# Agent attention into two expert layers on one core: the first product of layer 1 contracts over 128 rows in the place of 113

## The chip, the cores and the metric

The kernel runs on one core of one Trainium2 chip. The metric is the time of the execution on the device in microseconds (us). In this text PE is TensorE (its weight loads are shown apart, as PEld), DVE is VectorE, ACT is ScalarE, POOL is GpSimd and SP is SyncE, whose queue issues the large transfers.

## The reference

There are 12480 tokens of 128 channels and 49 agents. Attention runs first from the agents to the keys, then from the queries to the agents; two feed-forward layers with 2048 hidden units follow.

```
a2k = softmax(agents @ k.T / sqrt(128));  agent_v = a2k @ v          # 49 x 128
q2a = softmax(q @ agents.T / sqrt(128));  x = q2a @ agent_v          # 12480 x 128
h1  = relu(x @ w_in);   y = (s * h1 * h1 + b) @ w_out                # layer 1
h2  = relu(y @ w_in2);  out = (h2 * h2) @ w_out2                     # layer 2
```

## The kernel before

**Layer 1 from the agents.** Since `x @ w_in` is `q2a @ (agent_v @ w_in)`, the kernel forms `M = agent_v @ w_in` once (49 agents by 2048 hidden units) and layer 1 starts from the softmax weights themselves. Most products run on pairs of tiles: a value is split into a high part and a low remainder, and three products (low by high, high by low, high by high) are summed. In the first product of layer 1 the two parts of the softmax weights stand in one tile `X`: rows 0 to 48 hold one part and rows 64 to 112 the other, with rows 49 to 63 zero. `M` has the same layout, `Mh` the high parts and `Ml` the low ones, each once in rows 0 to 48 and again in rows 64 to 112. So two matmuls (`Ml` by `X`, `Mh` by `X`) do what would be four. The number of rows that they contract over is `KS = GAP + NA = 64 + 49 = 113`.

**Where the layout comes from.** `av` (high and low, 128 channels by 113 columns) holds the normalised agent values twice, at columns 0 and 64, on a ground of zeros that POOL writes at the start. `m_piece(i)` multiplies it with 512 hidden units of `w_in` (three matmuls, L338) into PSUM tile `ps_M`, and `split` (L112 on ACT, L113 on DVE) writes the pieces of `Mh` and `Ml`. There are four pieces: two before the main loop, two in steps 2 and 3. `q_stack(t)` transposes the softmax weights of a block of tokens into `ps_x` (L223) and copies its halves into the `X` tile of that block; there are two such tiles, which POOL sets to zero at the start (L378).

**The main loop.** The tokens lie in 28 blocks, 27 of 448 and a last one of 384. A block takes 8 steps (`NPR`), a step handles two of the 16 chunks of hidden units, and the steps of all blocks follow one another (`st`). In each step PE gets, in the order of the code:

- `up1(t, i)` (L543): 4 matmuls, `Ml` by `X` then `Mh` by `X` for two chunks, into a two-bank tile `ps_h`
- in some steps the work of another block: `q_transpose` (`ps_q`, L141) and `q_scores` (`ps_s`, L167) while the block to come is one of the first six, `q_scores_T` (`ps_sT`, L177, step 1) and `q_back` (`ps_b`, L192, step 2) for later ones, and `q_stack` (`ps_x`, L223) in step 6
- `up2` (L554): 6 matmuls of layer 2 for a block that is 11 steps behind, weights `wi2`
- `down` of layer 1 (L565 with `wo`): 6 matmuls; `down` of layer 2 (L565 with `wo2`): 6 matmuls
- after step 5 the four transposes of the output (`ps_o`, L592)

So a plain step is 22 matmuls with 128 by 448 or 113 by 448 moving elements: 4 at L543, 6 at L554, 12 at L565. `hidden` empties each `ps_h` tile: ACT takes relu (L530) and square (L531), DVE the split (L112, L113). The order on every engine is that of the code, written out by hand. After the last block's `up1` the loop drains: steps with L554 and L565 alone are left.

Of the kernel before, what the change touches and what calls it, by code (L numbers as in the profile page):

```python
# [10 lines left out]
F32R = mybir.dt.float32r  # L11
# [5 lines left out]
P = 128  # L17
# [21 lines left out]
def tile_agent_attention_two_moe(  # L39
# [14 lines left out]
    nc = tc.nc  # L54
    _, N, C = q.shape
    NA = agents.shape[1]
    DFF = w_in.shape[1]
# [4 lines left out]
    KS = GAP + NA  # L62
# [23 lines left out]
    const = ctx.enter_context(tc.tile_pool(name="const", bufs=1))  # L86
# [5 lines left out]
    ident = const.tile([P, P], F32, name="ident")  # L92
    ones = const.tile([P, P], F32, name="ones")
    aT = const.tile([P, GAP], F32, name="aT")
    M = [const.tile([KS, DFF], F32R, name=f"M{x}") for x in "hl"]
    av = [const.tile([P, KS], F32R, name=f"av{x}") for x in "hl"]
    s_sb = const.tile([P, 1], F32, name="s_sb")
    b_sb = const.tile([P, 1], F32, name="b_sb")
    ones_r = const.tile([P, P], F32R, name="ones_r")
# [5 lines left out]
    sTs = [const.tile([KS, 256], F32, name=f"sT{i}") for i in range(2)]  # L105
    aS = const.tile([P, KS], F32R, name="aS")
    halves = (0, slice(0, NA)), (1, slice(GAP, KS))
    Xs = [const.tile([KS, 512], F32R, name=f"X{i}") for i in range(2)]

    def split(dst, src, eng_lo, copy=nc.vector.tensor_copy):  # L110

        copy(dst[0], src)  # L112
        eng_lo.tensor_tensor(out=dst[1], in0=src, in1=dst[0].bitcast(F32), op=ALU.subtract)  # L113


    q_raw, qT, q_sT, q_e, q_st, X = {}, {}, {}, {}, {}, {}
# [216 lines left out]
    def m_piece(i):  # L333

        sl = slice(i * WC, (i + 1) * WC)
        ps = ps_m.tile([P, 512], F32, tag="m", name="ps_M")
        for z, (x, w) in enumerate(((av[0], wi[1]), (av[1], wi[0]), (av[0], wi[0]))):
            nc.tensor.matmul(out=ps[:KS], lhsT=x, rhs=w[:, sl], start=(z == 0), stop=(z == 2))  # L338
        split((M[0][:, sl], M[1][:, sl]), ps[:KS], nc.vector, nc.scalar.copy)

    with tc.manual_schedule():

        with tc.tile_pool(name="pre", bufs=1) as pre, tc.tile_pool(name="kp", bufs=2) as kp:
# [42 lines left out]
            ps = ps_m.tile([P, 512], F32, tag="m", name="ps_w")  # L386
            for i in range(16):
                nc.tensor.transpose(out=ps[:, :P], in_=ident, identity=ident)
            ps = ps_m.tile([P, 512], F32, tag="m", name="ps_a")
# [51 lines left out]
            ps = ps_m.tile([P, 512], F32, tag="m", name="ps_mt")  # L441
# [7 lines left out]
            ps = ps_m.tile([P, 512], F32, tag="m", name="ps_mb")  # L449
# [36 lines left out]
            for g, (_, p, j) in enumerate(kblocks):  # L486
# [6 lines left out]
                for i in range(j):  # L493
                    nc.tensor.matmul(
                        out=ps_av[:NA, :C + 1],
                        lhsT=S[:p, t0[g] + i],
                        rhs=vs[g][:p, i],
                        start=(g == 0 and i == 0),
                        stop=(g == NG - 1 and i == j - 1),
# [9 lines left out]
            ps = ps_m.tile([P, 512], F32, tag="m", name="ps_avT")  # L509
# [4 lines left out]
            for c0 in (0, GAP):  # L514
                nc.vector.tensor_tensor(
                    out=av[1][:, c0:c0 + NA], in0=ps[:, :NA], in1=av[0][:, c0:c0 + NA].bitcast(F32), op=ALU.subtract
                )
            for i in range(2):
                m_piece(i)
                fill(FM[i])  # L520
# [16 lines left out]
        def up1(t, i):  # L537
            n = blocks[t][1] * blocks[t][2]
            ps = ps_h.tile([P, 2, 512], F32, tag="h", name="ps_h1")
            for c in range(2):  # L540
                sl = slice((2 * i + c) * P, (2 * i + c + 1) * P)
                for z in (1, 0):
                    nc.tensor.matmul(out=ps[:, c, :n], lhsT=M[z][:, sl], rhs=X[t], start=(z == 1), stop=(z == 0))  # L543

# [54 lines left out]
        for st in range(total + L2 + LAG + 3):  # L599
            t, i = divmod(st, NPR)  # L600
# [8 lines left out]
            if st in M_AT:  # L609
                m_piece(2 + M_AT.index(st))  # L610
# [19 lines left out]
            t, i = divmod(st - L2, NPR)  # L630
            if 0 <= t < NB:
                up2(t, i)
            t, i = divmod(st - LAG, NPR)
# [4 lines left out]
            t, i = divmod(st - L2 - LAG, NPR)  # L638
# [4 lines left out]
            t, i = divmod(st - L2 - LAG - NPR, NPR)  # L643
# [32 lines left out]
```

## Time and profile before

| | |
|---|---|
| median of 3 runs | 1139.34 us (1139.15 to 1139.51) |
| the profiled execution | 1138.89 us |
| its span, first to last instruction | 1136.9 us |
| PE busy | 1113.1 us, 98% of the span |
| DVE, ACT busy | 979.4 and 943.5 us (86% and 83%) |
| mean granted TensorE clock | 0.993 of full speed |
| chain that ended last | PE 87%: L565 45%, L554 24%, L543 15% |

The span lies 2.0 us below the execution's own time, and the profiled execution 0.45 us below the median. Matmuls are pipelined, so a matmul's own duration is longer than the distance from its start to the start of the next one. That distance is called the pitch below; a group's pitch is read from the starts of two rows and the number of matmuls between them. In the chain view the durations of a group already add up to the distance between rows.

### The profile page before, as it was taken

How to read it: one execution, taken by the hardware profiler on the slowest of the kernel's cores; microseconds unless marked ns; L12 is line 12 of the kernel's file. 1: busy time of each engine (PE TensorE's matmuls, PEld its weight loads, DVE VectorE, ACT ScalarE, POOL GpSimd, SP SyncE). 2: the span in 40 equal slices, each digit the busy share in tenths (PEclk: the TensorE clock that was granted, in tenths of full speed). 3: DMA queues.
4: the chain of work that ended last, by engine and by line, in shares of the span. 5: the costliest groups of instructions: out<-in, count | busy, mean ns of one | idle time of the engine just before them, and what ended most of it. 6: DMA issues, size and time to landing. Idle time of an engine off the chain costs nothing.

```text
span 1136.9 us, 15468 instructions
## 1 busy us (share of the span) xinstructions
PE 1113.1 (98%) x5787; PEld 1026.2 (90%) x5787; DVE 979.4 (86%) x1425; ACT 943.5 (83%) x1183; POOL 38.3 (3%) x45
## 2 busy tenths in 40 slices
PE   8997899999999999999999999999999999999998
PEld 8986799999999999999999999999999999999997
DVE  5889998888888888888888888888888888888875
ACT  4646798888888888888888888888888888888875
POOL 1226100000000000000000000000000000000000
PEclk9899999999999999999999999999999999999999
DMA  8861009999999999999999999999999999800000
GB/s 309 246 200 35 1 1 23 15 15 7 15 15 15 13 10 15 15 15 8 15 15 15 7 15 15 15 15 8 15 15 15 8 15 15 12 1 9 9 10 15
DMA packets 1285730, 34.96 MB, mean 31 GB/s; under 512 B 1255239, under 2 KB 1281752, under 8 KB 1285656
## 3 DMA queue, kind: packets, MB, share of 16 engines
q1 hardware_dynamic: 1285368, 33.98, 116.0%
q8 instruction: 45, 0.74, 0.4%
q14 instruction: 29, 0.24, 0.1%
q10 hardware_dynamic: 288, 0.00, 0.0%
HBM read 27.58 MB, written 6.39 MB: 30 GB/s over the span
## 4 chain that ended last, share of the span: by engine, by line
PE 87%; DVE 6%; ACT 1%; issue 1%; POOL 0%; DVEq 0%; ACTq 0%
PE ps_y L565 45%; PE ps_h L554 24%; PE ps_h L543 15%; PE ps_o L592 1%; PE ps_sT L177 1%; DVE gh L112 1%; DVE gl L113 0%; ACT r L530 0%; DVE x L273 0%; DVE x L279 0%; DVE li L275 0%; PE ps_x L223 0%; POOL gl L113 0%; PE ps_b L192 0%; DVE ex L281 0%
## 5 line engine op out<-in xcount | busy, mean ns | idle before, releaser
L530 ACT ACTIVATE r<-ps_h 128x896 f32<-128x896 f32 (+1 forms) x448 | 408.7, 912 | 109.0 <-PE ps_h L543 77.7
L113 DVE TENSOR_TENSOR gl<-r,gh 128x896 fp32r<-128x896 f32 (+1 forms) x439 | 477.5, 1088 | 15.1
L531 ACT ACTIVATE r<-r 128x896 f32<-128x896 f32 (+1 forms) x448 | 426.6, 952 | 14.3
L112 DVE CAST gh<-r 128x896 fp32r<-128x896 f32 (+1 forms) x448 | 281.1, 628 | 108.8 <-ACT r L531 97.0
L554 PE MATMUL ps_h<-yh,wi2l 128*128 128x448 f32 (+1 forms) x448 | 169.1, 378 | 2.3 <-DVE yh L112 1.6
L565 PE MATMUL ps_y<-gl,woh 128*128 128x448 f32 (+1 forms) x448 | 163.3, 365 | 5.9 <-POOL gl L113 5.3
L543 PE MATMUL ps_h<-X,Ml 113*128 113x448 f32 (+1 forms) x448 | 166.4, 371 | 0.8 <-DVE Ml L113 0.8
L554 PE MATMUL ps_h<-yl,wi2h 128*128 128x448 f32 (+1 forms) x448 | 163.6, 365 | 0.1
L554 PE MATMUL ps_h<-yh,wi2h 128*128 128x448 f32 (+1 forms) x448 | 163.6, 365 | 0.0
L543 PE MATMUL ps_h<-X,Mh 113*128 113x448 f32 (+1 forms) x448 | 163.5, 365 | 0.0
L565 PE MATMUL ps_y<-gh,wol 128*128 128x448 f32 (+1 forms) x448 | 163.3, 364 | 0.0
L565 PE MATMUL ps_y<-gl,wo2h 128*128 128x448 f32 (+1 forms) x448 | 162.4, 362 | 0.6 <-DVE gl L113 0.6
L565 PE MATMUL ps_y<-gh,woh 128*128 128x448 f32 (+1 forms) x448 | 162.6, 363 | 0.0
L565 PE MATMUL ps_y<-gh,wo2l 128*128 128x448 f32 (+1 forms) x448 | 162.4, 362 | 0.0
L565 PE MATMUL ps_y<-gh,wo2h 128*128 128x448 f32 (+1 forms) x448 | 161.8, 361 | 0.0
L565 PEld LDWEIGHTS ps_y<-gl,woh 128*128 128x128 f32 x448 | 84.5, 189 | 13.5 <-POOL gl L113 6.8
L554 PEld LDWEIGHTS ps_h<-yh,wi2l 128*128 128x128 f32 x448 | 84.4, 188 | 9.7 <-issue 1.9
L554 PEld LDWEIGHTS ps_h<-yl,wi2h 128*128 128x128 f32 x448 | 84.9, 190 | 6.9 <-DVE yl L113 0.6
L543 PEld LDWEIGHTS ps_h<-X,Ml 113*128 113x128 f32 x448 | 84.5, 189 | 7.3 <-issue 1.2
L554 PEld LDWEIGHTS ps_h<-yh,wi2h 128*128 128x128 f32 x448 | 84.3, 188 | 7.0
L565 PEld LDWEIGHTS ps_y<-gh,wol 128*128 128x128 f32 x448 | 84.5, 189 | 6.4 <-ACT y L573 0.4
L565 PEld LDWEIGHTS ps_y<-gl,wo2h 128*128 128x128 f32 x448 | 84.1, 188 | 6.7 <-DVE gl L113 1.2
(122 smaller groups left out, 1025.5 us busy)
## 6 DMA issues: line engine op xcount, KB each, us to landing
kraw<-in_k_dram SPq DMA_DIRECT2D x12, 512.0 KB, 7.7
v<-in_v_dram SPq DMA_DIRECT2D x12, 512.0 KB, 7.3
q_raw<-in_q_dram SPq DMA_DIRECT2D x27, 224.0 KB, 36.3
out_dram<-o SPq DMA_DIRECT2D x27, 224.0 KB, 2.8
raw<-in_moe_w_in_dram SPq DMA_DIRECT2D x8, 512.0 KB, 7.0
raw<-in_moe_w_out_dram SPq DMA_DIRECT2D x8, 512.0 KB, 5.4
q_raw<-in_q_dram SPq DMA_DIRECT2D x1, 192.0 KB, 31.7
out_dram<-o SPq DMA_DIRECT2D x1, 192.0 KB, 2.3
```

Source lines behind the costliest of these rows:

```text
L112: copy(dst[0], src)
L113: eng_lo.tensor_tensor(out=dst[1], in0=src, in1=dst[0].bitcast(F32), op=ALU.subtract)
L177: nc.tensor.matmul(out=ps[:KS, :n], lhsT=aS, rhs=x[z][:, :n], start=(z == 1), stop=(z == 0))
L530: nc.scalar.activation(r[:, :, :n], ps[:, :, :n], AF.Relu)
L531: nc.scalar.activation(r[:, :, :n], r[:, :, :n], AF.Square)
L543: nc.tensor.matmul(out=ps[:, c, :n], lhsT=M[z][:, sl], rhs=X[t], start=(z == 1), stop=(z == 0))
L554: nc.tensor.matmul(out=ps[:, c, :n], lhsT=w[:, sl], rhs=y[:, :n], start=(z == 0), stop=(z == 2))
L565: nc.tensor.matmul(out=py[t][:, :n], lhsT=wz[:, m], rhs=g[:, c, :n], start=(m == 0 and z == 0), stop=(m == NCH - 1 and z == 2),)
L592: nc.tensor.transpose(out=po[:, i], in_=x[:, i * p:(i + 1) * p], identity=ident)
```

## The change

`M` and `X` become tiles of 128 partitions, `av` gets 128 columns. The zeros that POOL wrote on columns 49 to 63 of `av` and on rows 49 to 63 of `X` now also stand on columns and rows 113 to 127. `m_piece` computes all 128 rows of `M` (the new ones are zero) and splits them. Every matmul of `up1`, whose text is unchanged, then has 128 rows in the place of 113; the sums are the same.

```
-    M = [const.tile([KS, DFF], F32R, name=f"M{x}") for x in "hl"]
-    av = [const.tile([P, KS], F32R, name=f"av{x}") for x in "hl"]
+    M = [const.tile([P, DFF], F32R, name=f"M{x}") for x in "hl"]
+    av = [const.tile([P, P], F32R, name=f"av{x}") for x in "hl"]
...
-    Xs = [const.tile([KS, 512], F32R, name=f"X{i}") for i in range(2)]
+    Xs = [const.tile([P, 512], F32R, name=f"X{i}") for i in range(2)]
...
-            nc.tensor.matmul(out=ps[:KS], lhsT=x, rhs=w[:, sl], start=(z == 0), stop=(z == 2))
-        split((M[0][:, sl], M[1][:, sl]), ps[:KS], nc.vector, nc.scalar.copy)
+            nc.tensor.matmul(out=ps, lhsT=x, rhs=w[:, sl], start=(z == 0), stop=(z == 2))
+        split((M[0][:, sl], M[1][:, sl]), ps, nc.vector, nc.scalar.copy)
```

## Rows read from the trace of the kernel before

**Rows 1.** The page: its span, then busy time of three engines.
```profile
span 1136.9 us, 15468 instructions
...
PE 1113.1 (98%) x5787; PEld 1026.2 (90%) x5787; DVE 979.4 (86%) x1425; ACT 943.5 (83%) x1183; POOL 38.3 (3%) x45
```
**Rows 2.** Waits of PE, 130 to 1090 us: total us, times, longest.
```profile
PE ps_h L554 <- ACT r L530: 0.5, 1, 0.5
```
**Rows 3.** Chain that ended last, one block: start us, us, what.
```profile
504.35 0.81 PE ps_h L543 x4
...
505.36 1.22 PE ps_h L554 x6
...
508.98 0.82 PE ps_h L543 x4
509.80 1.23 PE ps_h L554 x6
511.02 2.40 PE ps_y L565 x12
513.42 0.82 PE ps_h L543 x4
...
519.23 1.23 PE ps_h L554 x6
```
**Rows 4.** The same chain where the loop drains.
```profile
1097.62 1.23 PE ps_h L554 x6
...
1101.09 1.20 PE ps_h L554 x6
...
1109.17 1.20 PE ps_y L565 x6
...
1117.72 1.06 PE ps_h L554 x6
...
1119.81 1.04 PE ps_h L554 x6
```
**Rows 5.** Timeline of PE early in the loop: start us, us of one.
```profile
89.86 0.37 PE L565 MATMUL ps_y<-gh,wol 128*128 128x448 f32 x1
...
91.10 0.36 PE L543 MATMUL ps_h<-X,Ml 113*128 113x448 f32 x1
```
**Rows 6.** The chain in one of the first blocks.
```profile
147.52 0.73 PE ps_s L167 x8
148.26 1.29 PE ps_h L554 x6
149.55 2.47 PE ps_y L565 x12
152.03 0.81 PE ps_h L543 x4
...
156.54 0.81 PE ps_h L543 x4
```
**Rows 7.** One group by form, 130 to 280, then 280 to 1090 us: busy, mean ns.
```profile
L565 PE MATMUL ps_y<-gl,wo2h 128*128 128x448 f32 x64 | 23.4, 365 | 0.0
...
L565 PE MATMUL ps_y<-gl,wo2h 128*128 128x448 f32 x352 | 127.6, 363 | 0.0
```
**Rows 8.** Weight loads by line and form: busy us, mean ns of one.
```profile
L543 PEld LDWEIGHTS ps_h<-X,Mh 113*128 113x128 f32 x448 | 84.9, 190 | 5.2
L554 PEld LDWEIGHTS ps_h<-yl,wi2h 128*128 128x128 f32 x448 | 84.9, 190 | 6.9 <-DVE yl L113 0.6
...
L338 PEld LDWEIGHTS ps_M<-wo2l,avh 128*113 128x113 f32 x4 | 0.7, 176 | 1.1 <-PE ps_y L565 1.0
```
**Rows 9.** POOL's memsets by line: busy us, mean ns of one.
```profile
L378 POOL MEMSET X<- 113x512 f32 x2 | 1.0, 526 | 0.0
L376 POOL MEMSET stack<- 128x256 f32 x2 | 0.6, 314 | 0.0
L376 POOL MEMSET sT<- 113x256 f32 x2 | 0.6, 311 | 0.0
```

## The prediction, made before the changed kernel ran

> **What bounds the kernel now.** I read the page first. PE is busy for 1113.1 of 1136.9 us; DVE and ACT stand at 86% and 83% [rows 1]. Next the waits of PE: in the 960 us from 130 to 1090 us there is one, of 0.5 us [rows 2]. So in the loop no other engine and no transfer holds PE back, and only what PE itself spends on a matmul can move the time. That is not a matter of busy time, which is full anyway; it is the pitch, so I read the chain that ended last as a clock. A plain step (the step at 508.98 us) is 0.82 us for four matmuls at L543, 1.23 for six at L554, 2.40 for twelve at L565, and the next step starts 4.44 us after this one [rows 3]. Per matmul that is 0.205, 0.205 and 0.200 us, although all 22 stream 448 columns. The question for this change is why the ten matmuls at L543 and L554 are slower than the twelve at L565, and whether the 113 rows are the cause.
>
> Three stretches bear on that. First, the drain: behind the last block's `up1` no L543 stands between the groups, and there six matmuls at L554 take 1.20 us, 0.200 each, as do six at L565 (at 1101.09 and 1109.17) [rows 4]. One step earlier, still right behind a group at L543, the same line took 1.23 (at 1097.62) [rows 4]. Second, before layer 2 has begun, a group at L565 comes right behind L543: six matmuls of 128 rows take 91.10 - 89.86 = 1.24 us [rows 5]. So the excess of 0.03 us is neither a property of L554 nor of the tile it writes: it falls on whatever stands behind L543. Third, a bad sign, one of the first blocks: behind eight small products (`ps_s`, L167) twelve matmuls at L565 take 2.47 us, 0.206 each, and the next step is again 4.51 us long (152.03 to 156.54) while L543 itself takes 0.81 [rows 6]. PE can thus run 128-row matmuls at 0.200 or at 0.206 us, and it stays with one of them for many matmuls. The later blocks hardly know the slow pitch: one group of L565 lasts 365 ns in the mean from 130 to 280 us and 363 from 280 to 1090 [rows 7]. What decides between the two I can't read from the trace.
>
> **The change part by part.**
>
> *L543, 224 steps, the last 8 of them 384 columns wide.* No instruction is added or removed. The rows go from 113 to 128. Bounds: if rows cost nothing, the pitches stay: 0. If the excess behind and inside L543 comes from the switch between 113 and 128 rows, a plain step falls to the price of an undisturbed stream, 22 x 0.200 = 4.40 us [rows 4], 0.04 less than now. The rows of the drain and of the early step are the nearest to an all-128-row loop, and I take the second value.
>
> A block has five steps with the plain sequence (0, 3, 4, 5, 7): 5 x 0.04 = 0.20 us. In the three others small products stand between L543 and L554, and these keep their fewer rows or columns. Behind transposes L554 has an excess without any L543 near: in the drain 1.06 against 1.04 us (at 1117.72 and 1119.81) [rows 4]. So of the 1.22 us behind `ps_x` (at 505.36) [rows 3], and behind `ps_b` alike, no more than about 0.01 can go. With 0.01 for each L543 group of 0.81 us (at 504.35) [rows 3], and up to 0.03 behind `ps_sT` (at 519.23), the three steps give 0.02 to 0.07; I take 0.04. The block gives 0.24 us.
>
> Blocks 5 to 26 repeat one pattern: 22 x 0.24 = 5.3 us. In blocks 0 to 4, where steps of both pitches occur [rows 6, 7], the gain lies between 0 and 5 x 0.24 = 1.2 us; I take half, 0.6. The last block and the drain give nothing. Sum: 5.9 us.
>
> *A rule against it.* The weight load of L543 with 113 rows takes 190 ns, that of L554 with 128 rows also 190 [rows 8]. The Trainium skill, page "TensorE: Matmul & The Clock Gate", section "LDWEIGHTS (loading the stationary operand)", says that the load's time goes with the columns of the stationary operand and not with its rows, and its section "Back-to-back issue gap" gives the spacing of matmuls as a function of the moving columns alone. By that rule this change moves nothing and the time stays 1139.3 us; by the rows above it is 5.9 us less. The trace agrees with the rule for the load, and disagrees with it for the spacing, by 2.5% between L554 behind L543 and L554 in the drain.
>
> *`m_piece`.* Twelve matmuls get 128 stationary columns in the place of 113. Their weight loads take 176 ns, those with 128 columns 190 [rows 8]: at most 12 x 0.014 = 0.17 us if none were hidden behind the stream of 512 columns; I take 0. The evictions keep 512 columns and get 15 more partitions. Partitions cost POOL nothing measurable (314 ns for 128, 311 for 113 at 256 columns) [rows 9]; ACT and DVE I take to be the same, 0.
>
> *POOL's start.* `X` keeps its columns; the two `av` memsets get 15 more columns, at 526/512 ns a column 0.015 us each [rows 9]. Cover: these tiles are first used some 75 us later. Without the cover it would be 0.03 us.
>
> *What is late next.* At 4.40 us a step PE still leads: 979.4 us of DVE work and 943.5 of ACT lie below the 1131 us that the span would have [rows 1], and in the loop neither holds PE now.
>
> *Against the runs.* The profiled execution took 1138.89 us, 2.0 more than its span; 1138.89 - 5.9 = 1133.0. It lay 0.45 below the median, so the forecast for the median is 1139.34 - 5.9 = 1133.4 us.
>
> **The rivals.**
>
> *A, rows cost nothing:* the excess comes from something else that only L543 brings (the same `X` streamed four times, one more group per step that waits for a `ps_h` tile). For it: the weight loads show no difference between 113 and 128 rows [rows 8], and streams of 128 rows at 0.206 exist. The Trainium skill's rule above speaks for it too. Against it: L554 also waits for a `ps_h` tile in the drain and has no excess. Time 1139.3 us.
>
> *B, the slow pitch takes hold:* the change removes the group that now stands between streams of 128 rows. In the slow step L543 costs 0.81 us, less than 4 x 0.206 = 0.82, and the fast pattern comes back behind L543 in every step of the later blocks; it may be what brings it back. If PE falls to 0.206 behind a small product and nothing pulls it out, a step is 22 x 2.47/12 = 4.53 us, 0.13 above the clean one [rows 6]. Place: the steps between the small products, from `ps_x` or `ps_b` on. The point from which it decides: 0.24/(8 x 0.13), or 23% of the steps, makes the gain zero. Half the steps slow gives (4 x 0.13 - 0.24) x 22 = +6.2 us, 1145.5 us; all of them (8 x 0.13 - 0.24) x 22 = +17.6, 1157 us. For it: the slow pitch is there in the first blocks and outlasts four steps. Against it: the whole drain, 128-row matmuls only, holds 0.200 behind waits and transposes, and from 280 us on the mean at L565 leaves hardly any room for slow groups [rows 7].
>
> *C, the change reaches further than I count:* the excess goes from the three mixed steps too, 8 x 0.04 x 27 = 8.6 us: 1130.7 us. The excess behind transposes in the drain speaks against it.
>
> **How the numbers follow.** A measurement of this kernel tells about 0.2% (2.3 us) from no change. The forecast and C are faster by more: 0.58 together (C 0.06). A, with the cases of B that land near zero: 0.20. B beyond that: 0.22, spread from 1141.6 to 1157. The range must reach from the faster cases over A into B until no more than 2 in 10 is left out: 1131 to 1144 us, where 1144 is B with some four steps in ten slow. It leaves out about 0.14 of B's chance above and 0.03 of C's below. The likeliest case alone has 1131 to 1136: its bounds are 22 x 0.22 + 0 and 22 x 0.27 + 1.2 us of gain, with about a microsecond for runs that differ.
>
> **What the profile after would show.** Right: plain steps of 4.40 us, L543 0.80 and L554 1.20 in the chain, the mean duration of L554 falling to that of L565; waits of PE as before. A: steps of 4.44 with the same 0.82 and 1.23 in spite of 128 rows. B: twelve matmuls at L565 at 2.47 in blocks behind 280 us. My prediction is wrong if the excess has another origin than the rows, or if the slow pitch, whose origin I don't know, takes more than a fifth of the steps. A clock that falls to half in another stretch, or new waits of PE, I don't expect: no instruction's place in a queue changes.

## The result, and the profile after

The changed kernel takes 1150.58 us in the median of 6 runs (1147.91 to 1150.76), the kernel before 1139.42 (6 runs, 1139.03 to 1142.58): 1.0084 times as long, 95% interval 1.0067 to 1.0100. By the medians it is slower by 11 us where 5.9 us less was forecast, and it lies outside the range. The runs of nearly every kernel here, those of the kernel before too, fall into two groups 2 to 3 us apart by the time ahead of the main loop (the first matmul at L543 starts at 81.4 us in the profile of before, at 84.3 in that of e2 below), so the 11 us overstate the loss: lower group against lower group it is about 9 us (1148.0 against 1139.3), as in the two spans. Kernels are compared by the ratio, which is taken on the same chip.

The page after, span and busy times:

```profile
span 1145.9 us, 15468 instructions
...
PE 1121.8 (98%) x5787; PEld 1023.9 (89%) x5787; DVE 980.4 (86%) x1425; ACT 943.4 (82%) x1183; POOL 38.4 (3%) x45
```

The span is 9.0 us longer, PE is busy 8.7 us more [rows 1], and the other engines did what they did before. The waits of PE from 130 to 1090 us are still one line:

```profile
PE ps_h L554 <- ACT r L530: 0.5, 1, 0.5
```

It equals [rows 2]: no wait was added. The weight loads of L543, 128 rows now, against those of L554 (busy us, mean ns of one):

```profile
L543 PEld LDWEIGHTS ps_h<-X,Mh 128*128 128x128 f32 x448 | 84.4, 188 | 5.1
...
L554 PEld LDWEIGHTS ps_h<-yl,wi2h 128*128 128x128 f32 x448 | 84.4, 188 | 7.0 <-DVE yl L113 0.6
```

They cost what they cost with 113 rows [rows 8]. So the loss, too, is in the pitch. The chain that ended last, one block of the changed kernel:

```profile
507.36 0.82 PE ps_h L543 x4
508.18 0.20 PE ps_x L223 x2
508.38 1.24 PE ps_h L554 x6
509.62 2.47 PE ps_y L565 x12
512.09 0.81 PE ps_h L543 x4
512.90 1.23 PE ps_h L554 x6
514.13 2.47 PE ps_y L565 x12
516.60 0.81 PE ps_h L543 x4
...
526.90 0.20 PE ps_b L192 x2
527.10 1.22 PE ps_h L554 x6
528.32 2.40 PE ps_y L565 x12
530.72 0.81 PE ps_h L543 x4
531.54 1.23 PE ps_h L554 x6
532.76 2.47 PE ps_y L565 x12
535.24 0.81 PE ps_h L543 x4
```

Read it against [rows 3]. A plain step is 516.60 - 512.09 = 4.51 us where it was 4.44. L543 and L554 cost what they did, 0.81 and 1.23; the twelve matmuls of L565, whose code, shapes and tiles are untouched, went from 2.40 to 2.47, the slow pitch that stood almost only in the first blocks before [rows 6, 7]. Behind `ps_b` the fast pitch comes back (2.40 at 528.32), and behind the next group of L543 it is gone again (2.47 at 532.76). Seven of the eight steps of this block are slow; in others the step with `ps_sT` is fast too, which leaves six: 6 x 0.07 x 22 blocks = 9.2 us, and 10.8 with seven, about the longer span. From the start of block 5 (its first L543, at 254.92 us before) to that of block 27 (at 1066.79) the kernel before takes 811.9 us and the changed kernel 820.7, 8.8 us more: nearly the whole loss lies in these 22 blocks. Over the later blocks as a whole, 280 to 1090 us, one group of L565 (busy us, mean ns of one):

```profile
L565 PE MATMUL ps_y<-gl,wo2h 128*128 128x448 f32 x348 | 127.5, 366 | 0.0
```

It was 363 [rows 7]. And where the loop drains, without L543, the changed kernel has the clean pitch just as before [rows 4]:

```profile
1110.15 1.20 PE ps_h L554 x6
```

### The profile page after: what moved, and what is told of

It reads as the page before. It is cut to its first block, busy times and chain, and to the rows that moved or that the text cites. A ratio compares the mean times of both kernels' runs of the same rounds, so it can differ in the third digit from the quotient of the medians.

```text
span 1145.9 us, 15468 instructions
## 1 busy us (share of the span) xinstructions
PE 1121.8 (98%) x5787; PEld 1023.9 (89%) x5787; DVE 980.4 (86%) x1425; ACT 943.4 (82%) x1183; POOL 38.4 (3%) x45
## 4 chain that ended last, share of the span: by engine, by line
PE 88%; DVE 6%; ACT 1%; issue 1%; POOL 0%; DVEq 0%; ACTq 0%
PE ps_y L565 46%; PE ps_h L554 23%; PE ps_h L543 15%; PE ps_o L592 1%; PE ps_sT L177 1%; DVE gh L112 1%; DVE gl L113 0%; ACT r L530 0%; DVE x L273 0%; DVE x L279 0%; DVE li L275 0%; PE ps_x L223 0%; POOL gl L113 0%; PE ps_b L192 0%; ACT r L531 0%
## 5 line engine op out<-in xcount | busy, mean ns | idle before, releaser
L554 PE MATMUL ps_h<-yh,wi2l 128*128 128x448 f32 (+1 forms) x448 | 168.2, 376 | 2.3 <-DVE yh L112 1.6
L565 PE MATMUL ps_y<-gl,woh 128*128 128x448 f32 (+1 forms) x448 | 164.6, 367 | 6.0 <-POOL gl L113 5.4
L543 PE MATMUL ps_h<-X,Ml 128*128 128x448 f32 (+1 forms) x448 | 166.0, 371 | 0.8 <-DVE Ml L113 0.8
L565 PE MATMUL ps_y<-gh,wol 128*128 128x448 f32 (+1 forms) x448 | 164.6, 368 | 0.0
L565 PE MATMUL ps_y<-gl,wo2h 128*128 128x448 f32 (+1 forms) x448 | 163.8, 366 | 0.6 <-DVE gl L113 0.6
L554 PE MATMUL ps_h<-yh,wi2h 128*128 128x448 f32 (+1 forms) x448 | 164.0, 366 | 0.0
L565 PE MATMUL ps_y<-gh,woh 128*128 128x448 f32 (+1 forms) x448 | 164.0, 366 | 0.0
L554 PE MATMUL ps_h<-yl,wi2h 128*128 128x448 f32 (+1 forms) x448 | 163.8, 366 | 0.1
L565 PE MATMUL ps_y<-gh,wo2l 128*128 128x448 f32 (+1 forms) x448 | 163.8, 366 | 0.0
L543 PE MATMUL ps_h<-X,Mh 128*128 128x448 f32 (+1 forms) x448 | 163.4, 365 | 0.0
L565 PE MATMUL ps_y<-gh,wo2h 128*128 128x448 f32 (+1 forms) x448 | 162.4, 362 | 0.0
L565 PEld LDWEIGHTS ps_y<-gl,woh 128*128 128x128 f32 x448 | 84.3, 188 | 15.6 <-POOL gl L113 6.8
L554 PEld LDWEIGHTS ps_h<-yh,wi2l 128*128 128x128 f32 x448 | 84.3, 188 | 9.3 <-issue 1.9
L543 PEld LDWEIGHTS ps_h<-X,Ml 128*128 128x128 f32 x448 | 84.4, 188 | 8.5 <-issue 1.2
L565 PEld LDWEIGHTS ps_y<-gl,wo2h 128*128 128x128 f32 x448 | 83.9, 187 | 8.8 <-DVE gl L113 1.2
L565 PEld LDWEIGHTS ps_y<-gh,wol 128*128 128x128 f32 x448 | 84.3, 188 | 8.2 <-ACT y L573 0.4
L565 PEld LDWEIGHTS ps_y<-gh,wo2l 128*128 128x128 f32 x448 | 83.9, 187 | 8.1 <-ACT oT L584 0.3
L565 PEld LDWEIGHTS ps_y<-gh,woh 128*128 128x128 f32 x448 | 84.2, 188 | 7.8
```

The lines of the kernel that those rows point to most:

```text
L554: nc.tensor.matmul(out=ps[:, c, :n], lhsT=w[:, sl], rhs=y[:, :n], start=(z == 0), stop=(z == 2))
L565: nc.tensor.matmul(out=py[t][:, :n], lhsT=wz[:, m], rhs=g[:, c, :n], start=(m == 0 and z == 0), stop=(m == NCH - 1 and z == 2),)
```

## The experiments

The prediction looked at rows. One other thing had changed, which no row of the profile shows: where the tiles lie. Tiles are allotted one behind the other in steps of 32 bytes a partition. `av` with 113 columns is 452 bytes, which takes 480; with 128 columns it takes 512. There are two, so every tile behind `av` moved by 64 bytes, and `M`, ahead of it, did not. The table gives two distances within 512 bytes: from where `M` begins to where the other weights (`wo`, `wi2`, `wo2`) do, and from the tiles streamed at L554 and L565 (`y`, `g`) to `X`. The plain step is the distance of two or three starts of L543 in the chain, from one profile of each kernel, and good to 0.01 us. The time of blocks 5 to 26 is taken as above, from the same profile; what happens ahead of the loop doesn't enter it. Ratios are to the kernel before on the same chip.

| kernel | rows | M to weights | y, g to X | plain steps, us | blocks 5 to 26, us | median, us | ratio, 95% interval |
|---|---|---|---|---|---|---|---|
| before | 113 | 32 | 320 | 4.44 | 811.9 | | |
| the changed kernel | 128 | 96 | 320 | 4.51, 4.52 | 820.7 | 1150.58 | 1.0084 (1.0067 to 1.0100) |
| e1_addresses_only | 113 | 96 | 320 | 4.42, 4.54 | 816.8 | 1143.78 | 1.0035 (1.0022 to 1.0049) |
| e2_rows_only | 128 | 32 | 320 | 4.43, 4.43 | 813.0 | 1140.60 | 1.0000 (0.9987 to 1.0014) |
| e3_weights_aligned | 128 | 128 | 320 | 4.46, 4.46 | 815.0 | 1143.42 | 1.0022 (1.0008 to 1.0036) |
| e4_m_misaligned | 128 | 128 | 320 | 4.45, 4.52 | 818.9 | 1147.67 | 1.0067 (1.0044 to 1.0089) |
| f1_same_offsets | 128 | 0 | 0 | 4.40, 4.40 | 807.7 | 1130.66 | 0.9909 (0.9893 to 0.9925) |
| f2_same_offsets_113 | 113 | 0 | 0 | 4.45, 4.45 | 813.5 | 1141.30 | 1.0003 (0.9991 to 1.0015) |
| f3_m_only | 128 | 0 | 320 | 4.42, 4.42 | 812.1 | 1138.74 | 0.9982 (0.9971 to 0.9994) |
| f4_x_only | 128 | 32 | 0 | 4.42, 4.42 | 810.4 | 1136.97 | 0.9967 (0.9952 to 0.9982) |
| g1_all_in_step | 128 | 0 | 0 | 4.40, 4.40 | 807.5 | 1135.18 | 0.9948 (0.9930 to 0.9966) |
| g3_weights_at_384 | 128 | 0 | 0 | 4.45, 4.45 | 813.8 | 1140.81 | 1.0009 (0.9997 to 1.0021) |
| g4_shifted_by_64 | 128 | 0 | 0 | 4.40, 4.40 | 807.3 | 1133.94 | 0.9943 (0.9924 to 0.9963) |
| g5_m_moved_along | 128 | 32 | 320 | 4.43, 4.44 | 815.1 | 1143.96 | 1.0023 (1.0010 to 1.0036) |
| h1_m_distance | 128 | 96 | 320 | 4.51, 4.52 | 820.9 | 1148.44 | 1.0072 (1.0048 to 1.0096) |
| h2_m_distance_113 | 113 | 96 | 320 | 4.42, 4.54 | 816.9 | 1146.70 | 1.0042 (1.0024 to 1.0059) |

Padding tiles get one memset of one column each on POOL at the start. In e1 to e4 the lines below the declarations have numbers up to four higher (L544 of e1 is L543).

**Rows or places.** e1 keeps the 113 rows and takes the places of the changed kernel:

```
-    av = [const.tile([P, KS], F32R, name=f"av{x}") for x in "hl"]
+    av_t = [const.tile([P, P], F32R, name=f"av{x}") for x in "hl"]
+    av = [x[:, :KS] for x in av_t]
```

> 113 rows as before, but av has 128 columns of which 113 are used, so that every tile behind it lies where it lies in the changed kernel (64 bytes on). Theory 1, the 128 rows of L543 turn the stream to the slow pitch: 1139 us, L565 2.40 us for twelve. Theory 2, the moved addresses do it: 1150 us, L565 2.47 us in the steps behind ps_x.

e2 is the changed kernel with `av` behind `X` and two tiles of its old size in its place:

```
-    av = [const.tile([P, P], F32R, name=f"av{x}") for x in "hl"]
+    hold = [const.tile([P, KS], F32, name=f"hold{x}") for x in "hl"]
...
     Xs = [const.tile([P, 512], F32R, name=f"X{i}") for i in range(2)]
+    av = [const.tile([P, P], F32R, name=f"av{x}") for x in "hl"]
```

> 128 rows as in the changed kernel, but every weight and X lies at its address of before (av stands behind X, two unused tiles hold its place; tiles behind X move by 1024 bytes). Theory 1 (rows): 1150 us. Theory 2 (addresses): 1139 us, or 1133 if the rows do what was forecast once the addresses are back.

Neither theory has it whole. The places alone cost 0.35%, with no row added; the rows alone cost nothing and, against the prediction, gave nothing: e2 still has a plain step of 4.43, and the 0.01 us that its plain steps gain is lost again behind `ps_x`, where L565 (here L568) is slow. Its chain from there:

```profile
509.03 2.47 PE ps_y L568 x12
511.50 0.81 PE ps_h L546 x4
512.32 1.22 PE ps_h L557 x6
513.53 2.40 PE ps_y L568 x12
515.93 0.82 PE ps_h L546 x4
```

Two plain steps of e1 in a row, in the chain:

```profile
510.37 0.81 PE ps_h L544 x4
511.18 1.22 PE ps_h L555 x6
512.39 2.40 PE ps_y L566 x12
514.79 0.81 PE ps_h L544 x4
515.61 1.24 PE ps_h L555 x6
516.85 2.48 PE ps_y L566 x12
```

The same 22 matmuls end once in the fast pitch and once in the slow one.

**Alignment.** e3 puts 32 bytes ahead of `wo` and 32 behind `wo2`; e4 puts them ahead of `M` and behind it.

```
+    pad0 = const.tile([P, 8], F32, name="pad0")
     wo = [const.tile([P, NCH, C], F32R, name=f"wo{x}") for x in "hl"]
...
+    pad1 = const.tile([P, 8], F32, name="pad1")
     stacks = [const.tile([P, 4, GAP], F32, name=f"stack{i}") for i in range(2)]
```

> The changed kernel with wo, wi2 and wo2 moved by 32 bytes, so that all weights begin at a multiple of 64 bytes as M does; before, M alone did. Theory 1 (rows): 1150 us, nothing moves. Theory 3, the pitch is disturbed where weights of one alignment follow weights of another: all 22 matmuls of a plain step at one pitch, 4.40 us (near 1131 us) or 4.53 us (near 1157 us), with no swing inside L543.

> The changed kernel with M moved by 32 bytes, so that it begins 32 bytes behind a multiple of 64 as wo, wi2 and wo2 do. Theory 1 (rows): 1150 us. Theory 3 (two alignments): one pitch in all groups of a plain step, 4.40 or 4.53 us; in e3 and here the same pitch if only the change of alignment counts, the better one where the alignment itself counts.

Theory 3 misses in both, and theory 1 in e3 (e4's time lies nearer to it). In e3 all weights begin at a multiple of 128 bytes, in e4 all 32 bytes behind one, and a plain step stays above 4.44. So agreement within 128 bytes is not enough. Left open was agreement over a longer stretch, since `M` lay 128 bytes from the other weights within 512, and `X` stood apart as before.

**All offsets alike.** f1 declares the small tiles first and pads so that `M` begins at 416 within 512 bytes as `wo` does, and `X` at 64 as `y` and `g` do. f2 is f1 with `M` and `X` of 113 rows. f3 and f4 each leave one of the two at its old offset.

```
     y1_bias = const.tile([P, 1], F32, name="y1_bias")
+    av = [const.tile([P, P], F32R, name=f"av{x}") for x in "hl"]; pad0 = const.tile([P, 112], F32, name="pad0")
+    M = [const.tile([P, DFF], F32R, name=f"M{x}") for x in "hl"]
     wo = [const.tile([P, NCH, C], F32R, name=f"wo{x}") for x in "hl"]
...
+    aS = const.tile([P, KS], F32R, name="aS"); pad1 = const.tile([P, 48], F32, name="pad1")
+    Xs = [const.tile([P, 512], F32R, name=f"X{i}") for i in range(2)]; pad2 = const.tile([P, 80], F32, name="pad2")
```

> 128 rows. All weights of the loop (M, wo, wi2, wo2) begin at one offset within 512 bytes, that of wo before (416), and all streamed tiles (X, y, g) at one, that of y and g before (64); before, M lay at 384 and X at 384. Theory 4, the swing of the pitch at L543 comes from the step from one offset to another, and rows count for nothing: no swing, 0.200 us for all 22 matmuls of a plain step, 4.40 us, near 1131 us. Theory 5, rows and addresses only pick one of two pitches by chance: any time from 1131 to 1157 us, with a swing at L543.

> As f1_same_offsets with 113 rows at L543. Theory 4: as f1, near 1131 us. If rows do count once the offsets agree: the swing of before stays (0.82 us for L543, 1.23 for L554), near 1139 us.

> 128 rows, M at the offset of the other weights, X at its own (384) as before. Theory 4 in the form that weights count: as f1. In the form that streamed tiles count: as e2_rows_only, 1139 to 1142 us.

> 128 rows, X at the offset of the other streamed tiles, M at its own (384) as before. Theory 4 in the form that streamed tiles count: as f1. In the form that weights count: as e2_rows_only, 1139 to 1142 us.

f1 hits theory 4. Its chain:

```profile
504.17 0.80 PE ps_h L543 x4
504.97 1.20 PE ps_h L554 x6
506.17 2.40 PE ps_y L565 x12
508.57 0.80 PE ps_h L543 x4
```

0.200 us for each of the 22 matmuls, 4.40 us a step: the drain's pitch, now with L543 in the loop. That its median, 1130.66, meets the 1131 us so closely is in part luck: blocks 5 to 26 take about 4 us less than before, and f1's profile also starts the loop early (first L543 at 79.9 us, f2's at 84.0). f2, the same offsets with 113 rows:

```profile
511.47 0.82 PE ps_h L543 x4
512.29 1.23 PE ps_h L554 x6
513.52 2.40 PE ps_y L565 x12
515.92 0.82 PE ps_h L543 x4
```

There the 0.82 and 1.23 of before are back, and by the ratio the time of before with them. So rows do count, but only once the offsets agree; the second half of theory 4, that they count for nothing, is wrong. f3 and f4 lie between, 4.42: the offset of the weights and that of the streamed tile each make a swing of their own.

**Agreement or place.** g4 is f1 with everything from `M` on 64 bytes further (a larger `pad0`). g3 is f1 with the weights alone 32 bytes back. g5 is the changed kernel with the declarations of `s_sb` and `b_sb` moved ahead of `M`, which moves `M` by 64 bytes and no weight behind it.

> f1_same_offsets with everything from M on 64 bytes further (weights at 480, streams at 128). Only agreement counts: 1131 us. If the 64 bytes themselves bring the slow pitch, as the shift from before to the changed kernel might have: 1150 us or more.

> f1_same_offsets with all weights of the loop 32 bytes back, at 384, a multiple of 64; still all alike. Theory 4 with only the agreement of offsets counting: 1131 us. If the offset itself counts too, as L554 and L565 in e3_weights_aligned suggest (0.201, 0.207, 0.199 us in turn, with weights at a multiple of 64): 22 x 0.0023 = 0.05 us more in each step, near 1142 us.

> The changed kernel with the two 4-byte scalars s_sb and b_sb ahead of M, so that M too moves by 64 bytes and all distances within 512 bytes are those of e2_rows_only; all but M, av and the scalars lie as in the changed kernel. If the loss came from the distance between M and the other weights (32 bytes before, 96 in the changed kernel): 1139 to 1142 us. If it came from where the tiles lie: 1148 to 1151 us.

g4 keeps 4.40, and 807.3 us in blocks 5 to 26 against f1's 807.7: the shift by 64 bytes is harmless to the loop where all make it together. g3 loses all of f1's gain though every offset still agrees; its chain:

```profile
511.51 0.81 PE ps_h L543 x4
512.32 1.21 PE ps_h L554 x6
513.53 2.43 PE ps_y L565 x12
515.96 0.81 PE ps_h L543 x4
```

No swing from one group to the next (0.81, 1.21 and 2.43 are all 0.202 a matmul), but an even pitch above 0.200: weights at a multiple of 64 bytes are worse here than weights 32 bytes off. (With the weights alone moved, their distance to the streamed tiles changed by the same 32 bytes; f1 and g4 share that distance too, so no run tells which of the two counts.) g5 takes the plain steps of the changed kernel from 4.52 to 4.44 and three quarters of the loss away by the ratio, 5.6 of 8.8 us in blocks 5 to 26; its median, 1143.96, lies above the expected 1142. A slow stretch behind `ps_x` stays, as the fourth line shows, with the fast pitch back one step later:

```profile
507.39 0.82 PE ps_h L543 x4
508.21 0.20 PE ps_x L223 x2
508.41 1.24 PE ps_h L554 x6
509.65 2.47 PE ps_y L565 x12
512.12 0.81 PE ps_h L543 x4
512.93 1.22 PE ps_h L554 x6
514.15 2.40 PE ps_y L565 x12
```

**The distance by itself.** h1 has 128 rows and every offset of e2, but `M` at 320 in the place of 384, which makes its distance to the other weights the 96 bytes of the changed kernel. h2 is h1 with 113 rows. Against f1:

```
-    av = [const.tile([P, P], F32R, name=f"av{x}") for x in "hl"]; pad0 = const.tile([P, 112], F32, name="pad0")
-    M = [const.tile([P, DFF], F32R, name=f"M{x}") for x in "hl"]
+    av = [const.tile([P, P], F32R, name=f"av{x}") for x in "hl"]; pad0 = const.tile([P, 88], F32, name="pad0")
+    M = [const.tile([P, DFF], F32R, name=f"M{x}") for x in "hl"]; pad1 = const.tile([P, 24], F32, name="pad1")
...
-    aS = const.tile([P, KS], F32R, name="aS"); pad1 = const.tile([P, 48], F32, name="pad1")
-    Xs = [const.tile([P, 512], F32R, name=f"X{i}") for i in range(2)]; pad2 = const.tile([P, 80], F32, name="pad2")
+    aS = const.tile([P, KS], F32R, name="aS")
+    Xs = [const.tile([P, 512], F32R, name=f"X{i}") for i in range(2)]; pad2 = const.tile([P, 128], F32, name="pad2")
```

> 128 rows, all offsets within 512 bytes as in e2_rows_only and before, but M at 320 in the place of 384: the distance from M to the other weights is the 96 bytes of the changed kernel. If this distance makes the loss: plain steps of 4.52 us as in the changed kernel, 1146 to 1151 us. If it takes the shift of the other tiles too: 4.44 us, 1139 to 1142 us as e2_rows_only.

> As h1_m_distance with 113 rows. If the distance alone counts: plain steps of 4.49 us and 1143 to 1146 us as in e1_addresses_only. If not: 4.44 to 4.45 us, 1139 to 1142 us as before.

Both meet the first case, h2 with a median 0.7 us above its range. h1's chain is that of the changed kernel, as is its time for blocks 5 to 26 (820.9 and 820.7 us):

```profile
512.36 0.81 PE ps_h L543 x4
513.17 1.23 PE ps_h L554 x6
514.40 2.47 PE ps_y L565 x12
516.87 0.81 PE ps_h L543 x4
```

h2 alternates between 4.42 and 4.54 as e1 does. With this, the place of `M` against the other tiles of the loop, set in h1 and taken back in g5, makes the loss. From which of these tiles the distance counts isn't shown: wherever `M` stands 96 bytes from the other weights (the changed kernel, e1, h1, h2) it also stands 64 bytes further from `X` than before (64 in the place of 0, within 512) and from `y` and `g`, and in e2 and g5 all three are as before.

**The scores' product in the same manner.** g1 is f1 with `aS` of 128 columns at the weights' offset and `qh` at the streams':

```
-    aS = const.tile([P, KS], F32R, name="aS")
+    aS = const.tile([P, P], F32R, name="aS")
...
-            nc.tensor.matmul(out=ps[:KS, :n], lhsT=aS, rhs=x[z][:, :n], start=(z == 1), stop=(z == 0))
+            nc.tensor.matmul(out=ps[:, :n], lhsT=aS, rhs=x[z][:, :n], start=(z == 1), stop=(z == 0))
```

> f1_same_offsets, and the product of the scores (L177) in the same manner: aS gets 128 columns, zeros behind 113, and the offset of the other weights (416), qh and ql that of the other streams (64). Theory 4, any step in rows, columns or offset disturbs the pitch, here too: the two matmuls at L177 take 0.40 us in the place of 0.59, and up to 22 x 0.2 = 4 us go, near 1127 us. If the scores' product is slow for another reason (the wait for ql): near f1_same_offsets, 1130 us.

It didn't help: blocks 5 to 26 take 807.5 us, f1's 807.7. The product still takes 0.60 us, and its weight load waits; the waits of PE's loads in g1 (total us, times, longest):

```profile
PEld ps_sT L177 <- DVE ql L113: 6.4, 22, 0.3
```

6.4/22 = 0.29 us a block: DVE brings `ql` late, and no offset mends that. f1, g1 and g4, all with 4.40 us a step, are the versions that beat the kernel before by more than f3 and f4 do: 0.5 to 0.9% by the ratio, 4 to 4.6 us in blocks 5 to 26.

## Why the prediction was wrong

**Right: what bounds the loop.** No wait was added, the loads are the same, DVE and ACT follow. All that moved is the pitch, and plain steps can reach 4.40 us: f1 shows them.

**Wrong: "If the excess behind and inside L543 comes from the switch between 113 and 128 rows, a plain step falls to the price of an undisturbed stream".** The term of 5 x 0.04 us a block rested on this. The rows are one of three causes: f2 against f1 (rows alone, 4.45 against 4.40), f4 against f1 (`M`'s offset alone, 4.42 against 4.40), f3 against f1 (`X`'s offset alone, 4.42 against 4.40). With the other two in place, as in e2, changing the rows gives 0.01 of the forecast 0.04 us a step, and blocks 5 to 26, where 5.3 us were to go, take 1.1 us more (813.0 against 811.9). Even f1, where every plain step has the 4.40, gains about 4 us there. The drain, on which I leaned, differed from the loop in all three at once: without L543 there are no 113 rows, and no `M` and no `X` either. It showed that L543 makes the excess, not which of its properties.

**Wrong: the cost of `av`.** "the two `av` memsets get 15 more columns, at 526/512 ns a column 0.015 us each" counted the work of the 15 columns and not their bytes. 2 x 32 bytes moved all later tiles away from `M`, and that makes the loss: h1 sets this place of `M` and is slow, g5 takes it back, and three quarters of the loss go. The rows have a share in it: with 113 rows the same place costs 0.35 to 0.42% (e1, h2), with 128 rows 0.72 to 0.84% (h1, the changed kernel).

**Rival B was the outcome, by another trigger.** Its price comes near, in part by luck: at six slow steps of a block's eight, (6 x 0.13 - 0.24) x 22 = 11.9 us more, 1151.2; measured 1150.6. That is 0.54 us a block, where the traces show 8.8/22 = 0.40: a slow step is 0.07 us longer than before, and the gain of 0.24 that the sum sets against it never came. Its place does not fit: it had PE fall to the slow pitch behind small products, with nothing to pull it out. Behind `ps_b` PE is fast; the slow pitch comes back one step later, behind L543, and with 128 rows and `M` where the changed kernel has it, it stays for most of a block (the changed kernel, h1). And rows alone, the change by its words, brought no such hold (e2).

**Rival A** (rows cost nothing) would have been right for the time of e2, the same rows at the old places; its reason holds only as long as the offsets differ (f1 against f2). The Trainium skill, page "TensorE: Matmul & The Clock Gate", section "LDWEIGHTS (loading the stationary operand)", has the load's time depend on columns alone, and the two traces agree (188 ns with 128 rows after, 190 with 113 before). For the spacing of matmuls f1 and f2 disagree with a rule by the moving columns alone: 4.40 against 4.45 us for 22 matmuls of 448 columns.

**What stays open.** The runs show that agreement in rows and in offsets gives an even pitch, of 0.200 us in f1, g1 and g4 and of 0.202 in g3. They don't show the mechanism; why `M` settles the loop into the slow pitch in one place and into the fast one in another, and whether its distance to the weights, to `X` or to `y` and `g` decides; what makes g3 slower; and whether 512 bytes are the length over which offsets have to agree. Only 128 and less are shown to be too short: e4 agrees there and takes 4.45 and 4.52 us a step, f3, with `M` in full agreement and `X` as far off as in e4, takes 4.42. The slow stretches behind `ps_x` and `ps_b`, which come and go from kernel to kernel (g5 against e2), weren't followed up. Each kernel has one profile.

## What to carry to other kernels

Where TensorE is the bound and never waits, read the pitch from the starts of its matmuls, group by group; if equal shapes run at unequal pitch, compare the rows of the operands and the offsets at which weights and streamed tiles begin. A tile that grows moves all tiles behind it: an experiment on a shape needs a partner that moves the places alone and one that holds them. Padding short operands to 128 rows was worth 5.8 us in 22 blocks here, 0.7% of them (f1 against f2), but only together with equal offsets.

## What the runs showed of the hardware that was not expected

- Matmuls of 128 rows, 128 columns and 448 streamed columns ran at two pitches, 0.200 and 0.206 us (twelve in 2.40 and in 2.47 us), and kept one of them over whole steps, with no wait of PE. The granted clock was 1.00 (2.4 GHz) in both: before in the steps at 527 and at 152 us, and in the changed kernel in the groups at 528.32 (2.40 us) and 532.76 (2.47 us).
- One pair of weight tiles, moved by 64 bytes against the other tiles of the loop, made the whole kernel 0.7% slower (h1 against e2, ratios 1.0072 and 1.0000, 820.9 and 813.0 us in blocks 5 to 26), with the same work in the same order.
- With all weights at a multiple of 64 bytes every group of a plain step ran at 0.202 us a matmul (g3), with all 32 bytes behind one at 0.200 (f1); the distance from weights to streamed tiles changed with it.
